# Reordering the loads and the first 50 microseconds of a gated attention and Mish kernel

## The chip, the cores and the metric

The kernel runs on one core of one Trainium2 chip. The metric is the device time of one execution in microseconds (us). Each such time is the span of the trace plus about 1.75 us. Every timed execution also reports the mean clock that was granted to TensorE (PE), as a share of full speed.

Engine names as the profile has them: PE is TensorE, ACT is ScalarE, DVE is VectorE, POOL is GpSimd, SP is SyncE (which here only issues DMAs). SPq and ACTq are the DMA issues of SP and ScalarE.

## The reference, cut to what matters

```python
def reference(A_x, A_wqkv, A_wo, B_x, B_w1, B_b1, B_w2, gate_w):   # S = 2048, D = 640, F = 1536, bf16
    x = A_x
    g = sigmoid((x * gate_w).sum(-1, keepdims=True))
    a = attention(x, A_wqkv, A_wo)        # 32 heads of 20, softmax over 2048 keys
    b = mish(x @ B_w1 + B_b1) @ B_w2
    return g * a + (1 - g) * b
```

The heavy part is 4 blocks of 512 queries x 8 groups of 4 heads x 2048 keys of exponentials.

## The kernel before

The kernel is generated by a planner in Python. It simulates five engines with estimated costs, chooses the next operation of each engine by those estimates, and then emits one fixed instruction order for each engine, with semaphore waits. The traces show what a fixed order costs: where the chip is later than the plan, an engine stands in front of the late operation even if later ones are ready (in e5 ScalarE stood for 4.31 us before the late gate row, though the scores of its next exponential were done at 39.22 us and that exponential started at 44.10).

The planner's cost of a DMA, and its way of keeping PE busy (dummy matmuls on a zero tile `ZD` whenever fewer than 4300 counted columns lie in the last 3.4 us):

```python
        if c.dma is not None:
            issue = 60.0
            start = max(self.now + issue + 1300.0, self.pipe.get(eng, 0.0))
            self.pipe[eng] = start + dur
    ...
        if sum(x[1] for x in w) >= 4300:
            pl.wake(60.0)
        elif ...:   # a matmul of ZD into OT or a spare bank
```

The loads. x is loaded transposed, in 4 column blocks of 5 tiles. The weights of head groups 0 and 1 ("part 0") come first on the ScalarE queue; the other three loads wait for the first x block:

```python
    for c in range(4):
        for ft in range(NFT):
            sp_q.append(loadx(c, ft))                       # DMA transposes
    act_q.append(load(WRAW[:, 1, :, 0:160], ..., ("wk", 0)))
    act_q.append(load(WRAW[:, 0, :, 0:160], ..., ("wq", 0)))
    act_q.append(load(WV[:, :, 1:161], ..., ("wv", 0)))
    act_q.append(load(WV[:, :, 0:1], gate_w..., ("gw",)))
    act_q.append(load(WV[:, :, 161:D + 1], ..., 614400, ("wv", 1), first))
    act_q.append(load(WRAW[:, 1, :, 160:D], ..., 614400, ("wk", 1), first))
    act_q.append(load(WRAW[:, 0, :, 160:D], ..., 614400, ("wq", 1), first))
    sp_q.append(...b1..., [("wq", 1)]); sp_q.append(...W1...); sp_q.append(...W2...); # then 4 x WO
```

Q and K weights are spread from 20 to 32 columns a head into zeroed tiles WQP and WKP. VectorE does part 0, GpSimd does part 1 and most of the clearing:

```python
    pool_q: memset WKP, WQP (groups 2 to 7); memset V_all; spread WK part 1; spread WQ part 1;
            memset WOG; identity matrix
    dve_fixed: memset ZD; memset WKP, WQP (groups 0, 1); memset OT; spread WK part 0; spread WQ part 0; b1
```

Exponentials: PE puts scores into PSUM, three banks (SA) and two banks (SB) in turn, ScalarE takes the exponential. Part of the units is computed on VectorE instead (seven kinds of instruction, XI to XE), in 2 of 8 quads from quad 9 on (4 of 8 from quad 128). The first group's Q and K wait for all 5 tiles of the first x block. The gate row g is stored to DRAM from SP and read back in another layout (GC); the normalisation of each group needs GC and goes through SP-issued DMAs (RC, RD, RB).

The softmax here doesn't subtract the row's maximum and nothing guards it: scores larger than these inputs give would overflow.

Of the kernel before, what the change touches and what calls it, by code (L numbers as in the profile page):

```python
# [7 lines left out]
BF16 = mybir.dt.bfloat16  # L8
# [6 lines left out]
P = 128  # L15
S = 2048
D = 640
NF = 1536
H = 32
DH = 20  # L20
NG = 8
NFT = D // P
# [21 lines left out]
class Cand:  # L44

    __slots__ = ("needs", "dur", "fn", "name", "dma", "mode", "cols", "also")

    def __init__(self, needs, dur, fn, name, dma=None, mode=None):
        self.needs, self.dur, self.fn, self.name, self.dma, self.mode = needs, dur, fn, name, dma, mode
        self.cols = 0  # L50
        self.also = []


class Planner:
# [26 lines left out]
    def take(self, eng, c):  # L81
        op = Op(eng, c.fn, [self.ev[n] for n in c.needs], c.dma, c.name)
        op.cols = c.cols
        dur = c.dur
        if c.dma is not None:
            issue = 60.0
            start = max(self.now + issue + 1300.0, self.pipe.get(eng, 0.0))
            self.pipe[eng] = start + dur
            op.end = self.now + issue
            op.vis = self.pipe[eng] + 700.0  # L90
        else:
            if eng == "PE":
                if self.pemode != c.mode:
                    dur += 100.0
                self.pemode = c.mode
            op.end = self.now + dur
            op.vis = op.end + self.LAT.get(eng, 100.0)
        self.free[eng] = op.end
        self.ops[eng].append(op)
        for n in c.also + ([c.name] if c.name is not None else []):  # L100
            assert n not in self.ev, n
            self.ev[n] = op
        heapq.heappush(self.heap, op.end)
        heapq.heappush(self.heap, op.vis)
        return op
# [117 lines left out]
def bass_gated_mix__softmax_full_mha__dense_activation_mish__prompt_kernel(  # L223
# [82 lines left out]

    xunits = [4 * n + 3 for n in range(9, NQ - 4) if n % 8 in ((1, 5) if n < 128 else (1, 3, 5, 7))]
    xunits = xunits[:len(xunits) // 2 * 2]
# [12 lines left out]
    NCH = len(chunks)  # L321
    assert NCH % 2 == 1

# [7 lines left out]
    def loadx(c, ft):  # L331
        return Cand([], 131072 / 130.0,
                    lambda h: h.dma_start_transpose(XT[:, ft, c * 512:(c + 1) * 512],  # L333
                                                    x_ap[c * 512:(c + 1) * 512, ft * P:(ft + 1) * P]),
                    ("x", c, ft), dma=f"d_x{c}")

# [3 lines left out]
    pool_q = []  # L340
    first = [("x", 0, NFT - 1)]
    for c in range(4):
        for ft in range(NFT):
            sp_q.append(loadx(c, ft))
    act_q.append(load(WRAW[:, 1, :, 0:160], wqkv[:, :, D:D + 160], 204800, ("wk", 0)))
    act_q.append(load(WRAW[:, 0, :, 0:160], wqkv[:, :, 0:160], 204800, ("wq", 0)))
    act_q.append(load(WV[:, :, 1:161], wqkv[:, :, 2 * D:2 * D + 160], 204800, ("wv", 0)))
    act_q.append(load(WV[:, :, 0:1], gate_w.rearrange("(f p o) -> p f o", p=P, o=1), 40000, ("gw",), allow_slow_non_contiguous=True))
    act_q.append(load(WV[:, :, 161:D + 1], wqkv[:, :, 2 * D + 160:3 * D], 614400, ("wv", 1), first))
    act_q.append(load(WRAW[:, 1, :, 160:D], wqkv[:, :, D + 160:2 * D], 614400, ("wk", 1), first))  # L350
    act_q.append(load(WRAW[:, 0, :, 160:D], wqkv[:, :, 160:D], 614400, ("wq", 1), first))
    sp_q.append(load(B1B[:, :], B_b1.rearrange("(f p) -> p f", p=P), 100000, ("b1",), [("wq", 1)], allow_slow_non_contiguous=True))
    sp_q.append(load(W1[:, :, :], B_w1.rearrange("(f p) c -> p f c", p=P), 1966080, ("w1",), [("wq", 1)]))
    sp_q.append(load(W2[:, :, :], B_w2.rearrange("(f p) c -> p f c", p=P), 1966080, ("w2",)))
    wo_v = A_wo.rearrange("(g j r) c -> j r g c", g=NG, j=4, r=DH)
    for j in range(4):
        sp_q.append(load(WOG[32 * j + 1:32 * j + 1 + DH, :, :], wo_v[j], 204800, ("wo", j), needs=[("wog0",)]))

# [12 lines left out]
    pool_q.append(Cand([], 3000.0, lambda h: pads(h, 2, NG), ("wpad", 1)))  # L371
    pool_q.append(Cand([], 600.0, lambda h: h.memset(V_all[:, :, :, 0:1], 1.0), ("v0",)))
    pool_q.append(Cand([("wpad", 1), ("wk", 1)], 2200.0, spread(1, 1), ("WK", 1)))
    pool_q.append(Cand([("wpad", 1), ("wq", 1)], 2200.0, spread(0, 1), ("WQ", 1)))
    pool_q.append(Cand([], 4000.0, lambda h: h.memset(WOG[:, :, :], 0.0), ("wog0",)))
    pool_q.append(Cand([], 200.0, lambda h: h.memset(IDF[:, :], 1.0), ("ones",)))
# [13 lines left out]
    class Fill:  # L390
        def __init__(self, kind, key, due, release, needs, mms, dur, evac, evdur, evneeds, evname):
# [3 lines left out]
            self.i = 0  # L395
            self.bank = None

    fills = []
# [5 lines left out]
    def add_q(qc, g):  # L404
# [5 lines left out]
        if gi >= 2:  # L410
# [5 lines left out]
                          600.0, prev, ("Q", qc, g)))  # L416
        fills[-1].mm = mm

    def add_fill(mm, *a):
        fills.append(Fill(*a))  # L420
        fills[-1].mm = mm

    def make_k(g, tc):
        def mm(h, b, i):
            return h.matmul(b[:, :], WKP[:, i, g * P:(g + 1) * P], XT[:, i, tc * 512:(tc + 1) * 512], start=(i == 0), stop=(i == NFT - 1))  # L425
        add_fill(mm, "K", (g, tc), g * 16 + 4 * tc, g * 16 - 28,
                 xdeps(tc) + [("WK", int(g >= 2))], NFT, 216.0,
                 lambda h, b: h.tensor_copy(KT[:, g, tc * 512:(tc + 1) * 512], b[:, :]), 600.0, [], ("K", g, tc))  # L428

    def make_v(p, tp):  # L430
# [226 lines left out]
    def f_cand(f):  # L657
        i = f.i
        needs = list(f.needs) if i == 0 else []
        if i == 0 and bank_free[f.bank] is not None:  # L660
            needs.append(bank_free[f.bank])
# [92 lines left out]
    def done_fill(f):  # L754
        b = MB[f.bank]
        dve_list.append((1, f.due, Cand([("mm",) + f.evname] + f.evneeds, f.evdur, lambda h: f.evac(h, b), f.evname)))
        bank_free[f.bank] = f.evname
        bank_user[f.bank] = None
        active.remove(f)
# [72 lines left out]
    if True:  # L832
        dve_list.append((1, 0, Cand([("ze",)], 80.0, lambda h: h.tensor_scalar_add(ZP[:, :], ZE[:, :], 1.0), ("zp",))))
        dve_list.append((1, 0, Cand([("zp",)], 170.0, lambda h: h.reciprocal(G[:, :], ZP[:, :]), ("g",))))
        dve_list.append((1, 0, Cand([("g",)], 80.0, lambda h: h.tensor_tensor(G1[:, :], ZE[:, :], G[:, :], ALU.mult), ("g1",))))
    sp_dyn.append(Cand([("g",)], 300.0, lambda h: h.dma_start(gdram[:].rearrange("(t p) -> p t", p=P), G[:, :],
                                                              allow_slow_non_contiguous=True), ("gd",), dma="d_gd"))
    for qc in range(NQC):
# [12 lines left out]
    ob = GL % 2  # L851
    TP = SA[:, QW:2 * QW]
    TB = SA[:, 2 * QW:2 * QW + QW // 2].bitcast(BF16)
    dve_list.append((0, 0, Cand([("VV", NQ - 1), ("OTN", GL - 1)], 600.0, lambda h: h.tensor_copy(OTC[ob][:, :], OT[:, :]), ("OTC", GL))))
# [6 lines left out]
    def tp2(h):  # L861
        for t in range(4):
# [13 lines left out]
               (lambda: MB[1][:, :], [13], 0, QW, lambda: [bank_free[1]]),  # L876
               (lambda: SB_[:, QW:2 * QW], [12, 13, 14, 15], QW, D, lambda: [("E", LC - 1)]),
               (lambda: SB_[:, 0:QW], [14], 0, QW, lambda: [("E", LC - 1)]),
               (lambda: SA[:, 0:QW], [15], 0, QW, lambda: [("E", LC)])]
    tail_parts = []  # L880
# [27 lines left out]
    for ri, tb, e in ((1, 13, "ACT"), (0, 12, "DVE"), (3, 14, "ACT"), (4, 15, "ACT")):  # L908
# [8 lines left out]
    dve_list.append((0, 4, Cand([("part", 2)], 600.0, lambda h: h.tensor_copy(  # L917
        BB1[:, 4:8, QW:D], SB_[:, QW:2 * QW].rearrange("p (t c) -> p t c", t=4)), ("fin", 3))))

# [61 lines left out]
```

## Time and profile before

| | before |
|---|---|
| timed runs | 903.23, 906.16, 905.5 us, median 905.5 |
| the profiled run | 898.24 us (span 896.5), granted clock 0.990 |

The profile's page, part 1: busy us, share of the span and instructions of each engine.

```profile
PE 807.3 (90%) x5879; PEld 262.9 (29%) x5945; DVE 727.7 (81%) x1229; ACT 860.2 (96%) x748; POOL 18.8 (2%) x13
```

ScalarE is nearly always busy, so time can only be won where it waits. The waits of ScalarE (who waited for whom: total us, times, longest):

```profile
ACT L771 <- issue: 10.7, 1, 10.7
ACT ETS L771 <- PE SA L452: 8.4, 8, 5.0
ACT W1F L911 <- PE MB L899: 6.1, 1, 6.1
ACT ETS L771 <- PE OT L648: 3.6, 5, 2.1
ACT ZE L783 <- DVE Z L444: 2.7, 1, 2.7
```

The longest one between the first exponential and the tail, in order of time (start, us, engine, line, operation, output<-inputs; in brackets the idle time before it and what ended it):

```profile
16.11 1.05 ACT L771 ACTIVATE ETS<-SB 128x1024 bf16<-128x1024 f32 x1
20.90 0.63 PE L425 MATMUL MB<-XT,WKV 128*128 128x512 bf16 x1 [5.06 <-DMA XT<-in_A_x_dram]
21.46 0.61 PE L452 MATMUL SA<-QT,KT 32*128 32x512 bf16 x3
22.12 1.45 ACT L771 ACTIVATE ETS<-SA 128x1536 bf16<-128x1536 f32 x1 [4.96 <-PE SA L452]
```

The K matmuls of the second column block wait for x; ScalarE waits for the scores behind them. The three matmuls took 0.61 us here where they took 0.39 us at 14 us: the clock is at half (PEclk 0.50 at 20 to 24 us). The spreads and GpSimd's clearing at the start:

```profile
3.90 0.46 DVE L365 COPY WKV<-HHF 128x800 bf16<-128x800 bf16 x1 [0.30 <-DMA HHF<-in_A_wqkv_dram]
4.04 3.48 POOL L369 MEMSET WQP<- 128x3840 bf16 x1
5.19 2.59 DVE L365 COPY WQP<-HHF 128x800 bf16<-128x800 bf16 x1 [0.83 <-DMA HHF<-in_A_wqkv_dram]
7.46 2.54 POOL L372 MEMSET V_all<- 128x512 bf16 x1
```

Two copies of one shape, 0.46 and 2.59 us: the second ends at 7.78 us, just after GpSimd's memset (7.52).

### The profile page before, as it was taken

What the parts mean: (1) busy time and instruction counts of PE and PEld (TensorE: products, weight loads), DVE (VectorE), ACT (ScalarE), POOL (GpSimd) and SP (SyncE); (2) the same over time, 40 slices, a digit from 0 to 9 for tenths busy, and PEclk for the clock granted to TensorE, in tenths of its full rate; (3) what the DMA queues carried; (4) which work ended last, traced back from release to release, by engine and by line L of the source; (5) the groups of instructions that cost most, each with busy time, mean ns of one, the idle gap of its engine ahead of it and who ended that gap; (6) DMA issues with size and microseconds to landing.
All of it is one profiled execution on the core that took longest, in us unless ns stands there. A gap on an engine that the chain in (4) does not pass through costs nothing.

```text
span 896.5 us, 14119 instructions
## 1 busy us (share of the span) xinstructions
PE 807.3 (90%) x5879; PEld 262.9 (29%) x5945; DVE 727.7 (81%) x1229; ACT 860.2 (96%) x748; POOL 18.8 (2%) x13
## 2 busy tenths in 40 slices
PE   6999999998999988799989989898979999999897
PEld 2333333322232222223323322222222233332223
DVE  3466756754899999689998999999948999998981
ACT  2899999999999999999999999999999999999995
POOL 6200000000000000000000000000000000000000
PEclk9999999999999999999999999999989999999999
DMA  9820000000000000000000000000000000000000
GB/s 192 226 26 25 2 13 13 14 13 12 3 13 14 14 13 14 8 20 21 21 11 17 30 14 13 14 14 13 7 7 14 13 1 14 21 20 21 21 14 30
DMA packets 37521, 22.05 MB, mean 25 GB/s; under 512 B 26705, under 2 KB 32849, under 8 KB 37457
## 3 DMA queue, kind: packets, MB, share of 16 engines
q1 hardware_dynamic: 32864, 18.68, 7.6%
q10 hardware_dynamic: 4592, 2.46, 1.2%
q8 instruction: 47, 0.77, 0.4%
q14 instruction: 18, 0.14, 0.1%
HBM read 15.37 MB, written 2.88 MB: 20 GB/s over the span
## 4 chain that ended last, share of the span: by engine, by line
ACT 50%; DVE 33%; PE 9%; DMA 5%; SPq 1%; issue 1%; ACTq 0%
ACT ETS L771 46%; DVE XI L462 7%; DVE XE L480 6%; DVE XS L475 3%; DVE XS L478 3%; DVE XF L474 3%; DMA RB<-rdram 3%; DVE XS L476 2%; DVE XF L477 2%; PE OT L648 2%; DMA rdram<-RR 1%; PE SA L452 1%; SPq L333 1%; PE MB L506 1%; ACT WKV L781 1%; ACT HHF L781 1%
## 5 line engine op out<-in xcount | busy, mean ns | idle before, releaser
L771 ACT ACTIVATE ETS<-SA 128x1536 bf16<-128x1536 f32 x366 | 589.7, 1611 | 11.9 <-PE SA L452 8.4
L771 ACT ACTIVATE ETS<-SB 128x1024 bf16<-128x1024 f32 x365 | 433.2, 1187 | 1.6 <-PE OT L648 1.0
L648 PE MATMUL OT<-ETS,V_all 128*21 128x512 bf16 x1828 | 197.7, 387 | 10.3 <-DVE XE L480 7.4
L462 DVE TENSOR_SCALAR XI<-MB 128x512 int32<-128x512 f32 x220 | 150.0, 683 | 58.2 <-PE SB L452 26.8
L452 PE MATMUL SA<-QT,KT 32*128 32x512 bf16 x1098 | 144.7, 387 | 40.9 <-ACT ETS L771 33.4
L452 PE MATMUL SB<-QT,KT 32*128 32x512 bf16 x730 | 143.1, 386 | 8.0 <-ACT ETS L771 5.0
L480 DVE SCALAR_TENSOR_TENSOR XE<-XI,XS 128x1024 uint16<-128x1024 int32 x110 | 134.1, 1219 | 2.1
L452 PE MATMUL MB<-QT,KT 32*128 32x512 bf16 x220 | 84.4, 386 | 5.9 <-ACT ETS L771 1.7
L731 PE MATMUL OT<-ZD 128*128 128x512 bf16 x291 | 86.7, 387 | 0.0
L648 PE MATMUL OT<-XE,V_all 128*21 128x512 bf16 x220 | 85.2, 387 | 0.0
L648 PEld LDWEIGHTS OT<-ETS,V_all 128*21 128x21 bf16 x1828 | 47.8, 89 | 127.4 <-issue 94.6
L452 PEld LDWEIGHTS SA<-QT,KT 32*128 32x128 bf16 x1098 | 35.6, 91 | 150.3 <-ACT ETS L771 143.6
L475 DVE TENSOR_TENSOR XS<-XF 128x1024 f16<-128x1024 f16 x110 | 75.6, 688 | 2.5
L478 DVE TENSOR_TENSOR XS<-XS,XF 128x1024 f16<-128x1024 f16 x110 | 75.6, 687 | 2.3
L474 DVE TENSOR_SCALAR XF<-XI 128x1024 f16<-128x1024 uint16 x110 | 75.6, 687 | 1.9
L487 PE MATMUL MB<-XT,W1F 128*128 128x512 bf16 x215 | 65.1, 384 | 3.4 <-DVE XI L462 1.2
L452 PEld LDWEIGHTS SB<-QT,KT 32*128 32x128 bf16 x730 | 34.3, 91 | 69.3 <-ACT ETS L771 55.6
L425 PE MATMUL MB<-XT,WKV 128*128 128x512 bf16 x140 | 45.0, 390 | 5.8 <-DMA XT<-in_A_x_dram 5.1
L408 PE MATMUL MB<-XT,WQP 128*128 128x512 bf16 x141 | 43.1, 383 | 5.3 <-DMA XT<-in_A_x_dram 2.0
L476 DVE TENSOR_SCALAR XS<-XS 128x1024 f16<-128x1024 f16 x110 | 46.1, 419 | 2.1
L477 DVE TENSOR_SCALAR XF<-XF 128x1024 f16<-128x1024 f16 x110 | 46.0, 418 | 0.0
L428 DVE CAST KT<-MB 128x512 bf16<-128x512 f32 x32 | 21.9, 684 | 29.3 <-PE MB L425 27.6
(86 smaller groups left out, 571.7 us busy)
## 6 DMA issues: line engine op xcount, KB each, us to landing
RB<-rdram SPq DMA_DIRECT2D x31, 256.0 KB
W1F<-in_B_w_dram SPq DMA_DIRECT2D x1, 1920.0 KB, 8.4
W<-in_B_w_dram SPq DMA_DIRECT2D x1, 1920.0 KB, 13.5
out_dram<-BB SPq DMA_DIRECT2D x8, 160.0 KB, 1.8
out_dram<-W1F SPq DMA_DIRECT2D x8, 160.0 KB, 1.9
HHF<-in_A_wqkv_dram ACTq DMA_DIRECT2D x2, 600.0 KB, 8.8
WOG<-in_A_wo_dram SPq DMA_DIRECT2D x4, 200.0 KB
WKV<-in_A_wqkv_dram ACTq DMA_DIRECT2D x1, 600.0 KB, 5.2
```

The lines of the kernel that those rows point to most:

```text
L452: return h.matmul(bank, KT[r, g, kt * P:(kt + 1) * P], QT[(qc * NG + g) % 2][r, :], start=True, stop=True)
L462: return h.tensor_scalar(XI[k // 2 % 2][:, (k % 2) * QW:(k % 2 + 1) * QW], b[:, :], SCALE * LOG2E * 65536.0, 127.0 * 65536.0, ALU.mult, AL ...
L474: lambda h: h.tensor_scalar(XF[:, :], XT2, 2.0 ** -16, -0.5, ALU.mult, ALU.add)),
L475: ("X2", [("X1", m)] + ([("XC", m - 1)] if m else []), 600.0, lambda h: h.tensor_tensor(XS[:, :], XF[:, :], XF[:, :], ALU.mult)),
L476: ("X3", [("X2", m)], 335.0, lambda h: h.tensor_scalar_add(XS[:, :], XS[:, :], -0.25)),
L477: ("X4", [("X2", m)], 335.0, lambda h: h.tensor_scalar(XF[:, :], XF[:, :], 128 * 0.078268, 128 * 0.34371, ALU.mult, ALU.add)),
L478: ("X5", [("X3", m), ("X4", m)], 600.0, lambda h: h.tensor_tensor(XS[:, :], XS[:, :], XF[:, :], ALU.mult)),
L480: lambda h: h.scalar_tensor_tensor(XE[:, e0:e0 + 2, :].rearrange("p u c -> p (u c)").bitcast(U16), XI[m % 2][:, :], 2.0 ** -9, XS[:, :], A ...
L487: return h.matmul(b[:, :], W1[:, i, fc * P:(fc + 1) * P], XT[:, i, tc * 512:(tc + 1) * 512], start=(i == 0), stop=(i == NFT - 1))
L648: ins = h.matmul(OT[32 * j:32 * j + DH + 1, :], V_all[:, kt, 4 * g + j, :], e, start=(kt == 0), stop=(kt == NKT - 1))
L731: c = Cand([("zd",)], 216.0, lambda h: h.matmul(OT[:, :], ZD[:, :], z, start=False, stop=False, skip_group_check=True), None, mode="F")
L771: return h.activation(ETS[:, e0:e0 + n, :].rearrange("p u c -> p (u c)"), src, AF.Exp, scale=SCALE)
```

## The change

The intent: let nothing delay x, start the first exponentials as early as x allows, and keep VectorE, SP and GpSimd out of ScalarE's way in the first 50 us. The core of the diff:

```diff
-            issue = 60.0
+            issue = c.issue                    # 500 by default
...
-    xunits = [4 * n + 3 for n in range(9, NQ - 4) if ...]
+    xunits = [4 * n + 3 for n in range(17, NQ - 4) if ...]
...
-        return Cand([], 131072 / 130.0, ... dma=f"d_x{c}")
+        cand = Cand([], 300.0, ... dma=f"d_x{c}_{ft}" if c == 0 else f"d_x{c}")
+        cand.issue = 1270.0
...
-    act_q.append(load(... ("wv", 1), first)); act_q.append(... ("wk", 1), first); act_q.append(... ("wq", 1), first)
+    sp_q.append(... ("wk", 1)); sp_q.append(... ("wv", 1)); sp_q.append(... ("wq", 1))     # behind the 20 x tiles
...  W1, WO, W2 now wait for ("OTN", 1), ("OTN", 2), ("OTN", 3); b1 waits for nothing
+    pool_q.append(... memset(WOG) ...)          # now ahead of the two spreads of part 1
...
+    def first_x(f):                             # for Q(0,0) and K(0,0)
+        f.needs = [n for n in f.needs if n[0] != "x"]
+        f.each = [[("x", 0, ft)] for ft in range(NFT)]
...
+        if f.evname == ("K", 0, 0):             # K(0,0) leaves PSUM by ScalarE
+            act_q.append(Cand([("mm",) + f.evname], 500.0, lambda h: h.copy(KT[:, 0, 0:512], b[:, :]), f.evname))
...
-    sp_dyn.append(Cand([("g",)], 300.0, ... dma_start(gdram ...
+    gate_q.append(Cand([("g",)], 10500.0, ... dma_start(gdram ...      # issued by ScalarE
...  the tail's PSUM banks follow the parity of the number of chunks
```

More of the change, by code (lines that the diff above doesn't have):

```diff
@@ L44 @@
 class Cand:
-    __slots__ = ("needs", "dur", "fn", "name", "dma", "mode", "cols", "also")
+    __slots__ = ("needs", "dur", "fn", "name", "dma", "mode", "cols", "also", "issue")
     def __init__(self, needs, dur, fn, name, dma=None, mode=None):
@@ L51, in __init__ @@
         self.also = []
+        self.issue = 500.0
 class Planner:
@@ L305, in quad @@
         return qc, g, kt
-    xunits = [4 * n + 3 for n in range(9, NQ - 4) if n % 8 in ((1, 5) if n < 128 else (1, 3, 5, 7))]
+    xunits = [4 * n + 3 for n in range(17, NQ - 4) if n % 8 in ((1, 5) if n < 128 else (1, 3, 5, 7))]
     xunits = xunits[:len(xunits) // 2 * 2]
@@ L321, in bass_gated_mix__softmax_full_mha__dense_activation_mish__prompt_kernel @@
     NCH = len(chunks)
-    assert NCH % 2 == 1
     pl = Planner()
@@ L331, in loadx @@
     def loadx(c, ft):
-        return Cand([], 131072 / 130.0,
+        cand = Cand([], 300.0,
                     lambda h: h.dma_start_transpose(XT[:, ft, c * 512:(c + 1) * 512],
                                                     x_ap[c * 512:(c + 1) * 512, ft * P:(ft + 1) * P]),
-                    ("x", c, ft), dma=f"d_x{c}")
+                    ("x", c, ft), dma=f"d_x{c}_{ft}" if c == 0 else f"d_x{c}")
+        cand.issue = 1270.0
+        return cand
     wqkv = A_wqkv.rearrange("(f p) c -> p f c", p=P)
@@ L340, in bass_gated_mix__softmax_full_mha__dense_activation_mish__prompt_kernel @@
     pool_q = []
-    first = [("x", 0, NFT - 1)]
-    for c in range(4):
-        for ft in range(NFT):
-            sp_q.append(loadx(c, ft))
     act_q.append(load(WRAW[:, 1, :, 0:160], wqkv[:, :, D:D + 160], 204800, ("wk", 0)))
@@ L348, in bass_gated_mix__softmax_full_mha__dense_activation_mish__prompt_kernel @@
     act_q.append(load(WV[:, :, 0:1], gate_w.rearrange("(f p o) -> p f o", p=P, o=1), 40000, ("gw",), allow_slow_non_contiguous=True))
-    act_q.append(load(WV[:, :, 161:D + 1], wqkv[:, :, 2 * D + 160:3 * D], 614400, ("wv", 1), first))
-    act_q.append(load(WRAW[:, 1, :, 160:D], wqkv[:, :, D + 160:2 * D], 614400, ("wk", 1), first))
-    act_q.append(load(WRAW[:, 0, :, 160:D], wqkv[:, :, 160:D], 614400, ("wq", 1), first))
-    sp_q.append(load(B1B[:, :], B_b1.rearrange("(f p) -> p f", p=P), 100000, ("b1",), [("wq", 1)], allow_slow_non_contiguous=True))
-    sp_q.append(load(W1[:, :, :], B_w1.rearrange("(f p) c -> p f c", p=P), 1966080, ("w1",), [("wq", 1)]))
-    sp_q.append(load(W2[:, :, :], B_w2.rearrange("(f p) c -> p f c", p=P), 1966080, ("w2",)))
+    for c in range(4):
+        for ft in range(NFT):
+            sp_q.append(loadx(c, ft))
+    sp_q.append(load(WRAW[:, 1, :, 160:D], wqkv[:, :, D + 160:2 * D], 614400, ("wk", 1)))
+    sp_q.append(load(WV[:, :, 161:D + 1], wqkv[:, :, 2 * D + 160:3 * D], 614400, ("wv", 1)))
+    sp_q.append(load(WRAW[:, 0, :, 160:D], wqkv[:, :, 160:D], 614400, ("wq", 1)))
+    sp_q.append(load(B1B[:, :], B_b1.rearrange("(f p) -> p f", p=P), 100000, ("b1",), allow_slow_non_contiguous=True))
+    sp_q.append(load(W1[:, :, :], B_w1.rearrange("(f p) c -> p f c", p=P), 1966080, ("w1",), [("OTN", 1)]))
     wo_v = A_wo.rearrange("(g j r) c -> j r g c", g=NG, j=4, r=DH)
     for j in range(4):
-        sp_q.append(load(WOG[32 * j + 1:32 * j + 1 + DH, :, :], wo_v[j], 204800, ("wo", j), needs=[("wog0",)]))
+        sp_q.append(load(WOG[32 * j + 1:32 * j + 1 + DH, :, :], wo_v[j], 204800, ("wo", j), needs=[("wog0",), ("OTN", 2)]))
+    sp_q.append(load(W2[:, :, :], B_w2.rearrange("(f p) c -> p f c", p=P), 1966080, ("w2",), [("OTN", 3)]))
     def spread(w, part):
@@ L372, in bass_gated_mix__softmax_full_mha__dense_activation_mish__prompt_kernel @@
     pool_q.append(Cand([], 600.0, lambda h: h.memset(V_all[:, :, :, 0:1], 1.0), ("v0",)))
+    pool_q.append(Cand([], 4300.0, lambda h: h.memset(WOG[:, :, :], 0.0), ("wog0",)))
     pool_q.append(Cand([("wpad", 1), ("wk", 1)], 2200.0, spread(1, 1), ("WK", 1)))
     pool_q.append(Cand([("wpad", 1), ("wq", 1)], 2200.0, spread(0, 1), ("WQ", 1)))
-    pool_q.append(Cand([], 4000.0, lambda h: h.memset(WOG[:, :, :], 0.0), ("wog0",)))
     pool_q.append(Cand([], 200.0, lambda h: h.memset(IDF[:, :], 1.0), ("ones",)))
@@ L396, in __init__ @@
             self.bank = None
+            self.each = None
     fills = []
@@ L417, in add_q @@
         fills[-1].mm = mm
+        if gi == 0:
+            first_x(fills[-1])
     def add_fill(mm, *a):
@@ L428, in make_k @@
                  lambda h, b: h.tensor_copy(KT[:, g, tc * 512:(tc + 1) * 512], b[:, :]), 600.0, [], ("K", g, tc))
+        if g == 0 and tc == 0:
+            first_x(fills[-1])
     def make_v(p, tp):
@@ L659, in f_cand @@
         needs = list(f.needs) if i == 0 else []
+        if f.each:
+            needs += f.each[i]
         if i == 0 and bank_free[f.bank] is not None:
@@ L755, in done_fill @@
         b = MB[f.bank]
-        dve_list.append((1, f.due, Cand([("mm",) + f.evname] + f.evneeds, f.evdur, lambda h: f.evac(h, b), f.evname)))
+        if f.evname == ("K", 0, 0):
+            act_q.append(Cand([("mm",) + f.evname], 500.0, lambda h: h.copy(KT[:, 0, 0:512], b[:, :]), f.evname))
+        else:
+            dve_list.append((1, f.due, Cand([("mm",) + f.evname] + f.evneeds, f.evdur, lambda h: f.evac(h, b), f.evname)))
         bank_free[f.bank] = f.evname
@@ L835, in bass_gated_mix__softmax_full_mha__dense_activation_mish__prompt_kernel @@
         dve_list.append((1, 0, Cand([("g",)], 80.0, lambda h: h.tensor_tensor(G1[:, :], ZE[:, :], G[:, :], ALU.mult), ("g1",))))
-    sp_dyn.append(Cand([("g",)], 300.0, lambda h: h.dma_start(gdram[:].rearrange("(t p) -> p t", p=P), G[:, :],
-                                                              allow_slow_non_contiguous=True), ("gd",), dma="d_gd"))
+    gate_q.append(Cand([("g",)], 10500.0, lambda h: h.dma_start(gdram[:].rearrange("(t p) -> p t", p=P), G[:, :],
+                                                                allow_slow_non_contiguous=True), ("gd",), dma="d_gd"))
     for qc in range(NQC):
@@ L851, in bass_gated_mix__softmax_full_mha__dense_activation_mish__prompt_kernel @@
     ob = GL % 2
-    TP = SA[:, QW:2 * QW]
-    TB = SA[:, 2 * QW:2 * QW + QW // 2].bitcast(BF16)
+    if LC % 2 == 0:
+        tbank = [SA[:, QW:2 * QW], SA[:, 2 * QW:3 * QW]]
+        pbank = [SB_[:, QW:2 * QW], SB_[:, 0:QW], SA[:, 0:QW]]
+    else:
+        tbank = [SB_[:, 0:QW], SB_[:, QW:2 * QW]]
+        pbank = [SA[:, 0:QW], SA[:, QW:2 * QW], SA[:, 2 * QW:3 * QW]]
+    TP = tbank[0]
+    TB = tbank[1][:, 0:QW // 2].bitcast(BF16)
     dve_list.append((0, 0, Cand([("VV", NQ - 1), ("OTN", GL - 1)], 600.0, lambda h: h.tensor_copy(OTC[ob][:, :], OT[:, :]), ("OTC", GL))))
@@ L876, in bass_gated_mix__softmax_full_mha__dense_activation_mish__prompt_kernel @@
                (lambda: MB[1][:, :], [13], 0, QW, lambda: [bank_free[1]]),
-               (lambda: SB_[:, QW:2 * QW], [12, 13, 14, 15], QW, D, lambda: [("E", LC - 1)]),
-               (lambda: SB_[:, 0:QW], [14], 0, QW, lambda: [("E", LC - 1)]),
-               (lambda: SA[:, 0:QW], [15], 0, QW, lambda: [("E", LC)])]
+               (lambda: pbank[0], [12, 13, 14, 15], QW, D, lambda: [("E", LC - 1)]),
+               (lambda: pbank[1], [14], 0, QW, lambda: [("E", LC - 1)]),
+               (lambda: pbank[2], [15], 0, QW, lambda: [("E", LC), ("E", LC - 1)])]
     tail_parts = []
@@ L917, in bass_gated_mix__softmax_full_mha__dense_activation_mish__prompt_kernel @@
     dve_list.append((0, 4, Cand([("part", 2)], 600.0, lambda h: h.tensor_copy(
-        BB1[:, 4:8, QW:D], SB_[:, QW:2 * QW].rearrange("p (t c) -> p t c", t=4)), ("fin", 3))))
+        BB1[:, 4:8, QW:D], pbank[0].rearrange("p (t c) -> p t c", t=4)), ("fin", 3))))
     def pick_dve():
```

## The prediction

> **What bounds the kernel now.** The page gives ScalarE 860 us busy of a span of 896.5 (96%), PE 90% (87 us of it dummy matmuls), VectorE 81%. From 60 to 880 us ScalarE is busy over 99% (windows): a 3-bank and a 2-bank exp together repeat every 2.23 to 2.26 us, 0.45 us a bank. So only ScalarE's idle time (36 us) can be won. By the timeline: 11.2 us before the first exp at 12.53 (without the 1.28 us table load), 5.0 us at 17.2 to 22.1, 1.4 us near 25, 2.7 us at 42.1 to 44.8, about 5 us scattered later, 6.1 us in the tail.
>
> **What the change does.**
> 1. *Weights behind x.* The 5.0 us gap is the wait for K(0,1), whose x tiles were issued by 12.7 but landed at about 20.4 while 1.8 MB of weights crossed at some 300 GB/s. Without them x lands about 1.7 us after its issue ends (tile 5: issue end 7.24, matmul at 8.97): column block 1 at about 15.5 and one more every 6.5 us. The exps need a block each 8 to 9 us. Gap gone. PE's 4.8 us idle there also halved its clock (0.50 at 20 to 24 us; scores 0.61 instead of 0.39 us)[...]; with that the 1.4 us gap goes too. Later weights arrive long before their use: harmless.
> 2. *Q/K follow x tile by tile.* Ten matmuls (2.5 us) after tile 5 become mostly two. But Q must wait for WQP, whose VectorE copy took 2.59 us against 0.46 for the equal WKP copy and ended at 7.78, beside GpSimd's memset[...]. So Q and K end near 9.8 instead of 11.3. K's evacuation on ScalarE (0.6 us, like the tail casts) runs beside Q's. First exp near 11.2: 1.3 us won. The table load should move ahead of the copy; if it stays behind it, 0.5 to 1 us is lost.
> 3. *No VectorE exps before quad 17.* Quads 9 and 13 go back to ScalarE: two banks, +0.9 us. But VectorE was in those exps just before the 2.7 us wait for Z; with them gone, and a plan whose x arrival (1.27 us an issue) matches the chip, I expect about 0.7 us of that wait to stay.
> 4. *Gate row from ScalarE.* An issue costs ScalarE 0.4 to 0.55 us, plus perhaps 0.5 us waiting for G. It frees SP, which bounds nothing.
> 5. *WOG cleared early*: nothing.
>
> **Sum.** Won 5.0 + 1.4 + 1.3 + 2.0 = 9.7; paid 0.9 + 0.9 = 1.8; about 7.5 to 8 us net, all on ScalarE's chain. Steady state, Mish phases and tail (the chunks' parity only swaps its banks) stay, with 1 to 2 us of noise from the re-planned order.
>
> **Prediction: 898 us, 894.5 to 902 (8 in 10). Faster by over 2%: 0.02; within 2%: 0.96; slower by over 2%: 0.02.**
>
> **What would show it.** Right: first exp near 11.2 us; no ScalarE wait over 1 us between 12 and 40 us; PE clock 1.0 at 18 to 26 us; the wait ahead of the ZE activation under 1 us; span near 889. Wrong on 1: a wait for K(0,1) to K(0,3) remains. Wrong on 2: first exp after 12 us. Wrong on 4: a ScalarE wait for G of over 1 us.
>
> **What would make it wrong.** A static plan that misjudges VectorE in the first 50 us puts a new wait in ScalarE's queue (for Z, G or a late K/V evacuation); PE stands before WQP; late weights make GpSimd's spreads collide with VectorE; a differently ordered middle adds or removes waits.

The sum came to 7.5 to 8 us.

## The result and the profile after

| | before | after |
|---|---|---|
| timed runs, us | 903.23, 906.16, 905.5, 903.33 | 890.54, 891.27, 890.11, 890.92 |
| median, us | 904.41 | 890.73 |
| span of the profiled run, us | 896.5 | 888.8 |
| its granted clock | 0.990 | 0.988 |

The ratio is 0.9847, 95% interval 0.9826 to 0.9868. Ratios in this document are the mean time of one kernel's fast runs over that of the other's fast runs of the same rounds, so not quite the ratio of the medians. The time fell outside the predicted range (894.5 to 902): the medians of before and after differ by 13.7 us, and 7.5 to 8 were forecast. Yet the two profiles differ by 7.7 us.

The profile after, part 1 and the waits of ScalarE:

```profile
PE 825.0 (93%) x5947; PEld 263.5 (30%) x5947; DVE 722.6 (81%) x1220; ACT 859.6 (97%) x750; POOL 18.8 (2%) x13
```

```profile
ACT W1F L932 <- PE MB L920: 6.6, 1, 6.6
ACT ETS L786 <- PE SA L462: 6.2, 9, 1.1
ACT KT L769 <- PE MB L433: 6.2, 1, 6.2
ACT L769 <- issue: 3.0, 1, 3.0
ACT ETS L786 <- PE OT L658: 2.4, 3, 1.3
```

The 5.0 us wait and the wait for Z are gone; between the first exponential and the tail nothing is longer than 1.3 us. The first exponential started at 11.58 instead of 12.53:

```profile
3.00 1.28 ACT L769 ACT_TABLE_LOAD   x1 [3.00 <-issue]
3.87 0.49 DVE L366 COPY WKV<-HHF 128x800 bf16<-128x800 bf16 x1 [0.27 <-DMA HHF<-in_A_wqkv_dram]
5.78 2.00 DVE L366 COPY WQP<-HHF 128x800 bf16<-128x800 bf16 x1 [1.41 <-DMA HHF<-in_A_wqkv_dram]
11.58 1.45 ACT L786 ACTIVATE ETS<-SA 128x1536 bf16<-128x1536 f32 x1 [0.56 <-PE SA L462]
```

The same stretch of both in the windows view (stretch; length, then the busy us of PE, PEld, DVE, ACT, POOL, each with the number of instructions; PEclk, DMA share, GB/s). First before, then after: ScalarE works 3.0 us more of these 10, and the clock is whole (1.00 instead of 0.74).

```profile
20.00:30.00 10.00, 9.04 (x58) 3.33 (x59) 1.94 (x4) 6.33 (x6) 7.09 (x5) 0.74 0.65 118
```

```profile
20.00:30.00 10.00, 9.40 (x80) 3.82 (x78) 3.05 (x8) 9.36 (x9) 0.00 (x0) 1.00 0.46 88
```

Of the prediction's own tests the start, the clock at 18 to 26 us, the wait ahead of ZE and the span near 889 came out; one wait (1.08 us, ahead of the exponential at 19.55) just missed "no wait over 1 us". So the traces say that the mechanism was seen nearly as it was, and the medians say that half of the gain was not. Two questions follow. Where do the other 6 us come from? And which parts of the change carry the gain?

### The profile page after: what moved, and what is told of

The parts are those of the page before. It is cut to its first block, busy times and chain, and to the rows that moved or that the text cites. A ratio compares the mean times of both kernels' runs of the same rounds, so it can differ in the third digit from the quotient of the medians.

```text
span 888.8 us, 14181 instructions
## 1 busy us (share of the span) xinstructions
PE 825.0 (93%) x5947; PEld 263.5 (30%) x5947; DVE 722.6 (81%) x1220; ACT 859.6 (97%) x750; POOL 18.8 (2%) x13
## 4 chain that ended last, share of the span: by engine, by line
ACT 71%; DVE 19%; PE 6%; SPq 2%; DMA 1%; issue 0%; ACTq 0%
ACT ETS L786 68%; DVE XI L472 4%; DVE XE L490 3%; DVE XS L488 2%; SPq L333 2%; DVE XF L484 2%; DVE XS L485 2%; ACT WKV L796 1%; ACT HHF L796 1%; DVE WKV L504 1%; DVE XS L486 1%; PE OT L658 1%; DVE XF L487 1%; PE SA L462 1%; PE OT L743 1%; DVE HHF L504 1%
## 5 line engine op out<-in xcount | busy, mean ns | idle before, releaser
L786 ACT ACTIVATE ETS<-SA 128x1536 bf16<-128x1536 f32 x366 | 606.7, 1658 | 9.0 <-PE SA L462 6.2
L786 ACT ACTIVATE ETS<-SB 128x1024 bf16<-128x1024 f32 x366 | 451.6, 1234 | 1.3 <-PE OT L658 0.9
L743 PE MATMUL OT<-ZD 128*128 128x512 bf16 x261 | 80.3, 394 | 0.0
L497 PE MATMUL MB<-XT,W1F 128*128 128x512 bf16 x240 | 73.0, 384 | 2.2 <-DVE XI L472 0.7
L433 PE MATMUL MB<-XT,WKV 128*128 128x512 bf16 x160 | 49.8, 384 | 2.4 <-DMA XT<-in_A_x_dram 1.5
L410 PE MATMUL MB<-XT,WQP 128*128 128x512 bf16 x160 | 50.6, 385 | 0.1
L487 DVE TENSOR_SCALAR XF<-XF 128x1024 f16<-128x1024 f16 x109 | 45.6, 419 | 0.0
```

What stands on the lines that cost most here:

```text
L487: ("X4", [("X2", m)], 335.0, lambda h: h.tensor_scalar(XF[:, :], XF[:, :], 128 * 0.078268, 128 * 0.34371, ALU.mult, ALU.add)),
L497: return h.matmul(b[:, :], W1[:, i, fc * P:(fc + 1) * P], XT[:, i, tc * 512:(tc + 1) * 512], start=(i == 0), stop=(i == NFT - 1))
L743: c = Cand([("zd",)], 216.0, lambda h: h.matmul(OT[:, :], ZD[:, :], z, start=False, stop=False, skip_group_check=True), None, mode="F")
L786: return h.activation(ETS[:, e0:e0 + n, :].rearrange("p u c -> p (u c)"), src, AF.Exp, scale=SCALE)
```

## The experiments

Eighteen kernels ran, each with 5 rounds, in five calls of two or four. Each call used its own chip, and all kernels of a call share 11 runs of before. All results were correct. "Clock" is the mean granted clock over a kernel's runs. The slow state appeared once (the first run of e3: 1091 us at a clock of 0.556); it is left aside.

| run | what | median (range), us | ratio to before | clock |
|---|---|---|---|---|
| e1 | before, copy | 900.6 (897.6 to 905.7) | 1.0014 | 0.984 |
| e2 | after, copy | 895.9 (890.8 to 898.4) | 0.9945 | 0.984 |
| e3 | before + weights behind x | fast runs: 912.1 (909.4 to 913.7) | 1.0132 | 0.982 |
| e4 | after, weights beside x | 890.9 (889.5 to 897.4) | 0.9908 | 0.989 |
| e5 | after, WOG cleared late | 897.5 (893.8 to 898.3) | 0.9924 | 0.985 |
| e6 | after, first spreads on ScalarE: "the control" | 892.3 (888.0 to 893.1) | 0.9867 | 0.988 |
| e7 | after, old DMA costs in the plan | 904.3 (897.8 to 908.9) | 0.9999 | 0.980 |
| e8 | before, new DMA costs | 900.6 (897.1 to 905.3) | 0.9979 | 0.985 |
| e9 | the control again | 890.1 (888.7 to 891.9) | 0.9867 | 0.990 |
| e10 | control, weights beside x | 891.8 (891.0 to 894.4) | 0.9889 | 0.989 |
| e11 | control, Q and K after the whole block | 895.9 (892.3 to 903.7) | 0.9938 | 0.983 |
| e12 | control, VectorE exps from quad 9 | 893.2 (892.9 to 895.7) | 0.9908 | 0.992 |
| e13 | before, more dummy matmuls | 904.0 (900.9 to 905.9) | 1.0023 | 0.984 |
| e14 | control, more dummy matmuls | 889.2 (885.2 to 892.6) | 0.9864 | 0.991 |
| e15 | control, old DMA costs | 899.3 (896.0 to 902.1) | 0.9974 | 0.981 |
| e16 | before + new costs + weights behind x | 919.9 (915.9 to 921.6) | 1.0195 | 0.979 |
| e17 | e16 + W1, WO, W2 held back | 907.5 (900.0 to 912.9) | 1.0067 | 0.979 |
| e18 | control, gate row from SP | 894.2 (892.9 to 899.0) | 0.9929 | 0.985 |

The 95% intervals of the ratios are about 0.0025 to 0.005 to either side, 2 to 5 us. The chips differ too: the medians of before were 898.6, 902.8, 903.0, 901.8 and 899.5. Each edit also re-runs the planner, which can change the order of the whole kernel and not only the part that is named.

### Copies of both kernels (e1, e2)

No edit.

> The kernel before, unchanged, to be profiled once more. The timed runs of before (903 to 906 us) lie 5 to 8 us above its profiled run (898.2); the timed runs of after lie within 1 us of its profiled run. Theory R (race): in before the x tiles and the 1.8 MB of weights on the other queue race, the profiled run was a lucky one, and a new profile of a run at about 904 us shows the ScalarE wait for the first K blocks at 9 to 12 us in place of 5.0. Theory E (elsewhere): the early wait stays at 5 us and the extra 5 to 8 us lie somewhere else (scattered waits, the middle, or time outside the span). Theory C (chip): on this chip all runs of before are near 898 us, and only chips differ. Ratio to before 1.000 within 0.003.

> The kernel after, unchanged, on the same chip as the others. Expected 890 to 891.5 us, ratio 0.985 to before, with a spread of under 1.5 us (theory R: no race is left, so it is steadier than before, whose spread should be 3 us or more).

*Measured.* Theory R (a race of x against the weights) fell: the profiled run of e1 took 905.65 us, 7.4 more than the profiled run of the prediction, and its early wait was shorter, 4.1 us. Theory C (only chips differ) fell too, since before ran from 896.6 to 906.9 us on this chip. The difference was in the middle (Theory E). The windows view around 400 us, first of the 896.5 us profile, then of e1's:

```profile
390.00:400.00 10.00, 8.98 (x69) 2.80 (x67) 7.05 (x13) 10.00 (x10) 0.00 (x0) 1.00 0.13 44
400.00:410.00 10.00, 9.05 (x75) 3.07 (x73) 9.86 (x17) 9.98 (x10) 0.00 (x0) 1.00 0.00 0
```

```profile
390.00:400.00 10.00, 9.09 (x63) 2.73 (x63) 7.13 (x13) 9.54 (x9) 0.00 (x0) 0.87 0.12 44
400.00:410.00 10.00, 10.00 (x47) 2.39 (x48) 6.97 (x11) 7.41 (x7) 0.00 (x0) 0.50 0.00 0
```

The same instructions, the same plan: in one run PE's clock halves for 13.7 us, PE is busy all the time and does 47 matmuls instead of 75, and ScalarE falls behind. The timeline of e1 gives the order of events: the clock halves at 397.44 us, and the slower matmuls (0.60 instead of 0.39 us) come before ScalarE's first wait (0.46 us, ended at 399.48), so here the clock is the cause of ScalarE's waits and not their effect.

```profile
398.83 0.60 PE L452 MATMUL SB<-QT,KT 32*128 32x512 bf16 x2
399.37 0.61 PE L648 MATMUL OT<-ETS,V_all 128*21 128x512 bf16 x4
399.48 1.02 ACT L771 ACTIVATE ETS<-SB 128x1024 bf16<-128x1024 f32 x1 [0.46 <-PE SB L452]
401.47 1.45 ACT L771 ACTIVATE ETS<-SA 128x1536 bf16<-128x1536 f32 x1 [0.97 <-PE SA L452]
```

The waits here add up to 4.0 us (seven of them, 399 to 412 us), and a second such stretch (half clock from 664 to 681 us) holds 3.7 us of waits, 3.2 more than the same place of the first profile. Together that is about the difference between the two spans (903.8 and 896.5).

The times and clocks of all runs say the same. Over 61 runs of before on five chips, time and mean clock correlate at -0.93, and the time rises by 6.2 us for each 0.01 of clock that is missing. Before in the call of e1, time (clock):

```
898.1(0.990) 901.6(0.982) 902.6(0.985) 897.4(0.988) 897.9(0.986) 896.6(0.992) 897.0(0.990) 906.9(0.975) 902.1(0.982) 898.6(0.988) 899.7(0.988)
```

After, on this chip, was not at 890 but mostly at 895 to 898. Its one profile (a run of 897.12 us) shows a cause: ScalarE's first exponential came at 19.28 us instead of 11.58.

```profile
3.86 3.73 DVE L366 COPY WKV<-HHF 128x800 bf16<-128x800 bf16 x1 [0.26 <-DMA HHF<-in_A_wqkv_dram]
4.04 3.30 POOL L370 MEMSET WQP<- 128x3840 bf16 x1
7.27 2.55 POOL L373 MEMSET V_all<- 128x512 bf16 x1
7.52 6.83 DVE L366 COPY WQP<-HHF 128x800 bf16<-128x800 bf16 x1
9.40 4.68 POOL L374 MEMSET WOG<- 128x5120 bf16 x1
14.41 1.46 PE L410 MATMUL MB<-XT,WQP 128*128 128x512 bf16 x3 [5.29 <-DVE WQP L366]
```

This is a lottery: one instruction of one program is short in one run and long in another. In the profile of after the WKP copy took 0.49 us (won), here 3.73 us (lost), each time beside GpSimd's memset of WQP. In nine profiles this copy on VectorE took 0.46 to 0.59 us six times (before, after, e1, e3, e4, e8) and 3.48 to 3.73 us three times (e2, e5, e7). In the long case it ended 0.25 us after the memset (7.59 against 7.34 us); in the short one the memset took 0.18 us longer (3.48 against 3.30). The WQP copy, 2.00 us in the profile of after, then lasted from 7.52 to 14.35 us here, past the change of memsets at 9.40 to 9.82 and until just after the WOG memset ended (14.08). The recorded starts do not tell the cases apart: the copy's is 3.87 us where it was short and 3.86 where it was long, the memset's 4.04 both times. What in the chip decides it, no run here shows.

*What follows.* Two sources of spread: half-clock stretches of PE, and VectorE's copies beside GpSimd's memsets. The typical run of before has more of the first than the profile that the prediction was read from: 17.9 us at half clock in that profile, 45.6 us in e1's.

### The copies beside GpSimd's memsets (e5, e6, e9)

e5 moves the WOG memset back behind the spreads of part 1. e6 takes the two part-0 spreads off VectorE:

```diff
-        Cand([("wk", 0), ("wpad", 0)], 500.0, spread(1, 0), ("WK", 0)),      # dve_fixed
-        Cand([("wq", 0), ("wpad", 0)], 500.0, spread(0, 0), ("WQ", 0)),
+    act_q.append(Cand([("wk", 0), ("wpad", 0)], 730.0, spread(1, 0), ("WK", 0)))
+    act_q.append(Cand([("wq", 0), ("wpad", 0)], 730.0, spread(0, 0), ("WQ", 0)))
```

> The kernel after with GpSimd's 4.7 us clearing of WOG back behind its two spreads. Theory L[...]: in the slow runs of after (e2) VectorE's copy into WQP ran from 7.52 to 14.35, to the end of GpSimd's memsets (14.08), because the WOG memset follows the V_all memset without a break; it cost 7.7 us of start. Without it the copy can last only to about 10.0, so the runs at 894 to 898 us go away: median 890 to 892 us, slowest under 895. Theory D (dips): the slow runs of after come from half-clock stretches in the middle as in e1, so this changes nothing: median 893 to 897, as e2.

> The kernel after, with the two first spreads (WKP and WQP, groups 0 and 1) done by ScalarE, which waits there anyway, in place of VectorE. Theory L: each takes about 0.8 us whatever GpSimd does; WQP is ready at about 6.5, Q and K end at about 9.5, first exp at about 11.0 in every run; 888 to 890.5 us with a spread under 2 us (unless a half-clock stretch adds 3 to 4). Theory D: like e2, 891 to 898.

> The kernel of e6 again, as the control of the next three, which each undo one part of the change in it (free of the GpSimd lottery, their differences can be read more finely). 888 to 893 us, ratio to before 0.985 to 0.990, no run over 894.

*Measured.* In e6 each spread took 0.86 us on ScalarE, beside GpSimd's memset of WQP (4.04 to 7.34 us), WQP was ready at 6.24 and the first exponential came at 11.31. Over the 12 runs of e6 and e9 no run was slower than 893.1 us, at a ratio of 0.9867 both times. In e5's profile the lottery was lost again (WKP copy 3.48 us), but WQP was done at 10.08 and the first exponential came at 13.22, as Theory L says. Still the runs did not get faster (897.5 us, where Theory L had 890 to 892), and the profile shows the late memset at a worse moment:

```profile
38.57 0.30 ACT L798 ACTIVATE ZE<-Z 128x16 f32<-128x16 f32 x1
38.82 4.37 POOL L376 MEMSET WOG<- 128x5120 bf16 x1
38.90 4.45 DVE L848 TENSOR_SCALAR ZP<-ZE 128x16 f32<-128x16 f32 x1 [0.70 <-ACT ZE L798]
44.10 1.45 ACT L786 ACTIVATE ETS<-SA 128x1536 bf16<-128x1536 f32 x1 [4.31 <-DVE G L849]
```

An addition on 16 columns took 4.45 us beside the WOG memset (1.07 us in the profile of after, 0.17 in e12's), and ScalarE, which has to issue the gate store in its own order, waited 4.3 us for it.

*What follows.* "WOG cleared early" is not idle work on an idle engine. In these two profiles it protects the gate row, and it raises the stake of the lottery at the start. The control has no copy in that place to lose, and both its profiles started by 11.31 us; it is used below because its runs are steadier.

### The order of the loads (e3, e4, e10, e16, e17)

e3 does this part alone in before; e4 and e10 undo it in after and in the control:

```diff
-    act_q.append(load(WV[:, :, 161:D + 1], ..., ("wv", 1), first))       # e4, e10: the reverse
-    act_q.append(load(WRAW[:, 1, :, 160:D], ..., ("wk", 1), first))
-    act_q.append(load(WRAW[:, 0, :, 160:D], ..., ("wq", 1), first))
+    sp_q.append(load(WRAW[:, 1, :, 160:D], ..., ("wk", 1)))              # behind the x tiles
+    sp_q.append(load(WV[:, :, 161:D + 1], ..., ("wv", 1)))
+    sp_q.append(load(WRAW[:, 0, :, 160:D], ..., ("wq", 1)))
```

e16 adds the new DMA costs of the planner to e3. e17 adds to e16 that W1, WO and W2 wait for the first normalised groups, as in after.

> The kernel before with one part of the change alone: the three 600 KB weight loads follow the 20 x tiles on the SP queue. Theory R: this takes most of the gain, 10 to 12 us (about 893 us, ratio 0.988), no ScalarE wait over 1.5 us between 13 and 35 us, PE clock 1.0 at 18 to 26 us. Theory of the prediction (fixed 5.0 + 1.4 us): 6 to 7 us, about 898 us, ratio 0.993.

> The kernel after with that part undone: the three weight loads go back to the ScalarE queue behind the first x block. Theory R: loses 9 to 12 us, about 901 us and as unsteady as before; first long ScalarE wait near 16 to 17 us, on K(0,1). Theory of the prediction: loses 6 to 7 us, about 897 us.

> The control with the three weight loads back on the ScalarE queue behind the first x block. Theory P (the prediction's sum): loses 5.0 + 1.4 us, 896 us or so. Theory N (e4 already showed 890.9 so): the loads beside x cost about 3 us early and their early arrival, with an honest plan, gives back as much elsewhere: within 2 us of the control.

> The kernel before with the new planner's costs and the three weight loads behind x, nothing else. The loads alone (e3) lost 13 us, the costs alone (e8) gained 0 to 2. Theory M: together they gain, since the plan then knows when the weights come: 893 to 897 us. Rival: late weights hurt this kernel whatever the plan knows (W1, W2 and WO are still queued right behind them): 905 us or more.

> The kernel of e16 with the loads of W1, WO and W2 held back until the first groups are normalised (as in after), and b1 no longer held. e16 lost 18 us to what stood behind the late weights: b1 landed at 60 us (6.8 us of VectorE), the gate row came back at 70 us behind 4 MB of W1 and W2, and the second group's normalisation made ScalarE wait 8.2 us at 94 us. Theory Q (queue): these waits go, 893 to 898 us remain, with the waits at the start (WOG clear, Z) still there. Rival: the late weights for groups 2 and up themselves cost it, over 905 us.

*Measured.* Undone in after it costs nothing: e4 is 5.0 us faster than e2 by median, on the same chip, but e2's profile lost the lottery and e4's won it (WKP copy 0.51 us), so this pair can't say more. Undone in the control it costs 1.75 us of median (e10 against e9, same chip), within the noise, as Theory N says, although e10's profile shows the predicted wait for the second x block at its longest:

```profile
25.56 1.45 ACT L787 ACTIVATE ETS<-SA 128x1536 bf16<-128x1536 f32 x1 [6.69 <-PE SA L463]
```

That profiled run was e10's slowest (894.4). e4's profile had 3.24 us in this place. Against it, the control itself waits 1.08, 0.54, 1.14 and 0.30 us in its first 60 us where e10 waits only once more (0.43).

Done in before it loses 12 us alone (e3) and 18 with the new costs (e16). The late weights push everything that stood behind them; that is read from e16, since e3's only profile is slow. In e16 W2 and the read-back of the gate row kept SP issuing until 70 us. The first group's sums left PSUM at 62.56 (OTC), but the last DMA of its normalisation (RB) was issued only at 95.99, and ScalarE waited 8.2 us for the accumulator (OT) that this holds up:

```profile
59.02 10.98 SPq L843 DMA_DIRECT2D GC<-gdram  x4
62.56 0.68 DVE L812 COPY OTC<-OT 128x512 f32<-128x512 f32 x1
95.99 0.55 SPq L825 DMA_DIRECT2D RB<-rdram  x1
102.71 1.45 ACT L774 ACTIVATE ETS<-SA 128x1536 bf16<-128x1536 f32 x1 [8.23 <-PE OT L651]
```

With W1, WO and W2 held back the same way from OTC to RB took 6 us (57.51 to 63.55) instead of 33, and this wait is gone (e17, 12 us faster than e16 by median, on another chip). Part of the 33 us is the plan's own doing: it charges W1 and W2 to the SP queue and so puts VectorE's step for the first group late in its order (93.83). What the profile of e17 shows next is the same stretching again: GpSimd's spreads and its WOG clear, which in before were over by 27 us, now run to 43 us, into VectorE's first exps. One of these took 4.66 us beside the WOG clear, where its mean in the first profile of before is 0.42 us.

```profile
38.66 4.64 POOL L378 MEMSET WOG<- 128x5120 bf16 x1
38.92 4.66 DVE L480 TENSOR_SCALAR XF<-XF 128x1024 f16<-128x1024 f16 x1
44.07 0.21 ACT L786 ACTIVATE ZE<-Z 128x16 f32<-128x16 f32 x1 [7.99 <-DVE Z L447]
```

*What follows.* The headline part of the change is worth little by itself and does harm without its companions. Holding back the later loads takes the largest wait away (e17); that WOG early and no exps on VectorE before quad 17 do the rest is likely from e17's waits, but no run added them to e17. Theory R fell, and e16's Theory M (honest costs rescue it) fell too. Of e17's Theory Q the named wait went, but the kernel stayed 0.7% slower than before.

### The plan's DMA costs (e7, e8, e15)

```diff
-        self.issue = 500.0              # e7 and e15 in after and in the control; e8 does the reverse in before
+        self.issue = 60.0
...
-        cand.issue = 1270.0             # an x tile
+        cand.dur = 131072 / 130.0
```

> The kernel after, with the planner's old costs of a DMA (60 ns an issue, x tiles at about 1 us each on the pipe) in place of 1270 and 500 ns an issue. Theory M (model): the plan's honest arrival times are most of the gain; with the old ones the order of PE and VectorE runs ahead of the data and ScalarE waits 5 to 15 us in the first 60 us: 897 to 905 us. Theory of the prediction: the order of the loads is what matters, the plan only 1 to 2 us: 890 to 898 as e2.

> The kernel before with the new planner's costs alone (no load moved, no instruction added). Theory M: gains 4 to 7 us, 892 to 896 us; the 2.7 us wait for Z and the 1.4 us near 25 us shrink, a wait of 3 to 5 us for K(0,1) stays. Theory of the prediction: 1 to 2 us, about 898 us.

> The control with the planner's old costs of a DMA. Theory M with K: the plan then runs ahead of the chip, more waits in the first 70 us (4 to 6 us more than the control) and more half-clock stretches: 896 to 902 us, clock under 0.985. Rival: e7's loss was GpSimd's lottery alone, and this stays at 889 to 892.

*Measured.* With the old costs the control loses about 10 us (e15 0.9974; 10.1 us of median above e14, the control with more dummies, on the same chip, 9 above e9 on another). e15's profile shows waits of 3.69, 0.88 and 1.06 us at 22 to 33 us and 1.86 us at 57 us, and its clock is lower (0.981). e7 shows the same and the lost lottery on top of it (first exponential at 18.91 us). Alone in before the new costs win nothing clear (e8: 0.9979, interval 0.9943 to 1.0014). Theory M holds in the new kernel and fell for the old one.

### Q and K tile by tile, VectorE's exps, the gate row (e11, e12, e18)

```diff
-        if gi == 0: first_x(fills[-1])                                  # e11, with the same for K and
-        if f.evname == ("K", 0, 0): act_q.append(...)                   # K's evacuation back on VectorE
...
-    xunits = [4 * n + 3 for n in range(17, NQ - 4) ...                  # e12
+    xunits = [4 * n + 3 for n in range(9, NQ - 4) ...
...
-    gate_q.append(Cand([("g",)], 10500.0, ...gdram...                   # e18
+    sp_dyn.append(Cand([("g",)], 300.0, ...gdram...
```

> The control with the first Q and K after the whole x block and K evacuated by VectorE, as in before. Theory P: first exp near 12.5 in place of 11.3, loss 1.2 us.[...]

> The control with VectorE's exps from quad 9 again. Theory P: ScalarE has 0.9 us less work, but about 2 us more of waits for Z, G or late evacuations in the first 60 us: net loss about 1 us. Rival: the wait for Z was the old plan's fault, so the loss is nil or a gain of 0.9 us.

> The control (after, first spreads on ScalarE) with the gate row stored from the SP queue again. Theory P (the prediction): gains the 0.9 us that the issue and the wait for G cost ScalarE: 889 us. Rival: with the loads held back SP is free anyway, and nothing changes: within 0.7 us of the control's 890.1, whose wait for G was 1.1 us in e9 and 0 in e14.

*Measured.* e11: the first exponential came at 12.94 instead of 11.29, a shift of 1.65 us, but the median rose by 5.8 us, and the runs spread from 892.3 to 903.7 with clocks down to 0.973. Its profile has a wait of 2.55 us at 54 us (e9 has 0.30 there, but e6, also the control, 1.58), and its runs have lower clocks; how the rest divides between them is not shown.

e12: ScalarE waited once for long, as VectorE's exp instructions, one of them stretched to 2.56 us beside GpSimd's spread (mean in the profile of after: 0.42 us), came late:

```profile
36.32 2.19 POOL L366 COPY WQP<-HHF 128x2400 bf16<-128x2400 bf16 x1 [1.84 <-DMA HHF<-in_A_wqkv_dram]
36.37 2.56 DVE L486 TENSOR_SCALAR XS<-XS 128x1024 f16<-128x1024 f16 x1
43.02 1.45 ACT L786 ACTIVATE ETS<-SA 128x1536 bf16<-128x1536 f32 x1 [6.80 <-PE OT L658]
```

The median is 3.1 us above e9's, although e12's clock is the highest of all (0.992).

e18: 0.9929 against 0.9867, some 5 us lost (on another chip, and at a lower clock, 0.985 against 0.988 to 0.990). SP issued in the order of its program: it stood for the landing of the gate row, issued at 38.77, until it issued the read-back (GC) at 49.38, and only then, at 51.78, the first normalisation's load (RC), whose input (OTC) VectorE had copied by 44.52. VectorE stood for RC, and PE and ScalarE for VectorE:

```profile
49.38 2.35 SPq L855 DMA_DIRECT2D GC<-gdram  x4
51.78 0.55 SPq L826 DMA_DIRECT2D RC<-OTC  x1
53.67 0.25 DVE L829 RECIPROCAL RC<-RC 128x16 f32<-128x16 f32 x1 [5.42 <-DMA RC<-OTC]
55.27 1.02 ACT L786 ACTIVATE ETS<-SB 128x1024 bf16<-128x1024 f32 x1 [4.30 <-PE SB L462]
```

In after the gate row was stored by ScalarE, SP issued RC at 46.04 and stood for the landing only afterwards, with GC at 50.47. Both the prediction's view and its rival (nothing changes) fell.

### More dummy matmuls (e13, e14)

```diff
-        if sum(x[1] for x in w) >= 4300:
+        if sum(x[1] for x in w) >= 5300:        # e13, in before; e14: 4800, in the control
```

> The kernel before with one constant of its planner changed: dummy matmuls are put in until 5300 instead of 4300 counted columns lie in 3.4 us (472 dummies instead of 313). Theory K (clock): what sets a 904 us run of before apart from an 897 us run is half-clock stretches of PE; over 39 runs of before the time falls by 6.6 us for each 0.01 of mean clock. So the clock rises to 0.988 or more in every run, the slow runs go away: 896 to 899 us, slowest under 901. Rival: the low clock goes along with something else that also makes the run slow; more dummies only load PE further: 900 to 907 us, as before.

> The control (after, first spreads on ScalarE) with 4800 instead of 4300 counted columns (405 dummies instead of 315). Theory K: the control's clock is already 0.987 to 0.992, so at most 1 to 2 us are won: 888 to 890 us. Rival: more dummies get in PE's way and cost: 891 us or more.

*Measured.* e13 is a miss for Theory K as it was put: 159 more dummies in before raised neither the clock (0.984) nor the speed. Its profiled run had six half-clock stretches, 31 us before the one at the end. e14's median was 0.8 us below e9's, with one run at 885.2 (clock 0.995), which is no clear gain.

*What follows.* That the low clock costs time is shown by e1's order of events and by the 61 runs. That it can be cured by a higher threshold of dummies is not so.

The kept clock records show what goes before a half-clock stretch, which the experiments did not look at. The stretches of one clock that begin and end inside these traces last whole multiples of 3.41 us (half clock in the first profile of before: 6.83 us from 18.47, 3.41 from 363.22, 6.83 from 660.18; in that of after: 10.24 us from 353.60 and from 653.97), so the traces were cut into steps of this length from 12 to 880 us. In the first profile of before half clock followed three of the 248 steps at full clock, those in which PE was busy for 0.79, 0.61 and 0.03 us; in that of after two of 248 (0.05 and 0.57 us); in all others of the two PE was busy for 1.84 us or more. Counted over the 19 fast profiles, the clock halved after every one of the 44 steps at full clock in which PE was busy for less than 1.36 us; after 20 of the 50 with 1.36 to 2.39 us; and after one of the 4576 with more. That one is e1's at 397 us (2.7 us busy; 2.87 in the same place of the first profile, where the clock held), so the trace does not say why this stretch began. These are counts of what went together in these traces; no run changed PE's work in such a step alone. Of the 67 stretches that begin before 880 us, 41 begin near 360 or 660 us, where ScalarE runs Mish and PE waits for it (4.4 and 6.0 us in the first profile of before). e13's added dummies did not fill these places: four of its six stretches still follow less than 1.4 us of work.

The losses above mix time at a given clock with a lower clock. An estimate for the parts at one clock: shift every fast run to a clock of 0.988 by 6.2 us for each 0.01 (within the 18 kernels the slope is also 6.2). Before is then at 898.9 us, the control at 891.2, e10 at 892.4, e18 at 892.9, e11 at 893.5, e15 at 895.0 and e12 at 895.9. So more than half of what e11, e15 and e18 lost is clock. Some of that clock may be the part's own doing (e15's profile has half clock from 22 to 33 us, among its waits), so this is the smaller reading of each part.

## Why the prediction was wrong, point by point

- **The step that failed: "Prediction: 898 us", which is 905.5 less 7.5.** The sum of 7.5 to 8 us was read from a profile of a 898.24 us run and subtracted from the median of runs that took 905.5 us. The prediction held both bases: its "span near 889" is 896.5 less 7.5, measured 888.8, and means a time of about 890.7, which is what came, and not 898. The missing term is the half-clock stretches beyond those of the profiled run (17.9 us there, 45.6 us in e1's run of 905.65 us). At equal clock the sum is right: the 11 later runs of before whose clock read 0.988 averaged 898.3 us; the three of the first four runs of after at 0.988 averaged 890.9. That is 7.4 us. (In e2 two more runs read 0.988: one took 890.75, one, at 894.63, seems to have lost the lottery.) The remaining 6 us between the first medians are most likely clock: 6 us of time is 0.01 of clock by the slope above, an estimate from the later runs. It is not shown for these runs themselves, since the clocks of the first four timed runs of before were not recorded; a slow chip alone could add up to some 4 us by the medians. The 13.7 us were also a lucky draw: before was slower than later, after at its fastest (its profile won the lottery); on e2's chip the ratio was 0.9945. The warning was on the table: 898.24 beside 903 to 906.
- **Weights behind x, "won 5.0 + 1.4".** The gap and the half clock at 20 us went, as forecast (1.00 instead of 0.74). As a part it is worth 1 to 2 us in the control, within the noise, and costs 12 to 18 in before. "Later weights arrive long before their use: harmless" was wrong: GpSimd's spreads and clear moved into VectorE's first exps (e17), and the SP queue behind them moved too (e16). The prediction had this only in its list of what might go wrong.
- **Q and K tile by tile, "first exp near 11.2: 1.3 us won".** 11.58 in the profile of after, 11.3 in the control, and the table load moved ahead as hoped. But it is so only when the lottery is won; where it was lost, 19.28 (e2). The prediction saw one 2.59 us copy beside a memset and took it for a fixed cost. Undone, this part costs 5.8 us of median, about 2 at equal clock, against the 1.3 of the prediction.
- **VectorE exps from quad 17, "+0.9 us" against "2.0 us" of the wait for Z.** The sign was right, the size was 3.1 us of median (e12; 4.7 at equal clock), against a net of 1.1, and the wait for Z went wholly.
- **Gate row from ScalarE, "frees SP, which bounds nothing", cost 0.9.** Wrong in sign: some 5 us lost when undone (e18), about 2 of them at equal clock.
- **WOG early, "nothing".** Wrong in both directions (e2, e5).
- **The plan's costs** were only a remark under the third point. Undone in the control they cost about 10 us of median, the largest single part (about 4 at equal clock, where e12's part is as large); alone in before they gave nothing clear. The parts are not additive.
- **What stays open.** Why some plans (before, e7, e8, e15, e16, e17) draw low clocks of 0.972 to 0.980 in two or more runs and others (e4, e6, e9, e10, e12) never under 0.985 was not taken apart by any run. The traces give a lead, steps in which PE hardly works, above all beside Mish; no run filled just those. Why e1's stretch at 397 us began is open too.

A version that beats before and is steadier than after: the control, ratio 0.9867 with a range of 888.0 to 893.1 us over 12 runs, where the ten runs of after lie between 890.1 and 898.4.

## What to carry to other kernels

Before you subtract a saving that you read from a trace, ask which draw the trace is: compare its time and clock with the median's, and read the saving at equal clock. A short VectorE copy beside long GpSimd memsets was a lottery here (WKP 0.46 to 0.59 or 3.48 to 3.73 us, WQP up to 6.83); try such copies on another engine (on ScalarE they took 0.86 us each beside the same memsets, e6), and look where GpSimd's work moves to when its inputs come later. Where the clock reads low, look for the steps in which PE idles (here half clock followed all 44 steps of 3.41 us with under 1.36 us of PE work). In a statically ordered kernel, a part that "bounds nothing" is judged by what stands behind it on the same queue (e18: RC 7 us after its input), so undo each part by itself in the finished kernel, not only alone in the old one.
